# Gated linear attention and a cosine router: keys and queries in runs of two tokens, turned by small products

## The chip, the cores and the metric

The kernel runs on one core of a Trainium2 chip. The metric is device time in microseconds (us), the median of several executions; lower is better. The engines are TensorE (PE, matrix products, with its weight loads shown apart as PEld), VectorE (DVE), ScalarE (ACT), GpSimd (POOL) and SyncE (SP), which here issues DMA transfers. They run side by side, each through its own list of instructions in order, and wait for one another by semaphores.

## The reference, cut to what matters

Two blocks follow each other, all in fp32. The first is a recurrence with a decay per channel: 4 batches, 8 heads, 768 tokens, 48 channels.

```python
for t in range(S):
    state = alpha[:, :, t, :, None] * state + np.einsum('bhd,bhe->bhde', k[:, :, t], v[:, :, t])
    y[:, :, t] = np.einsum('bhd,bhde->bhe', q[:, :, t], state)
```

(The update is the outer product of k and v of the token, 48x48 for each head.) Its output, with the heads side by side, is x: 3072 tokens of 384. The second block sends each token to one of 8 experts:

```python
logits = (x / |x|) @ (expert_emb / |expert_emb|).T / tau
expert = argmax(logits);  gate = softmax(logits)[expert]
out = gate * (relu(x @ w1[expert]) @ w2[expert])      # w1 384x1024, w2 1024x384
```

## The kernel before, in words

**Stage 1** is the recurrence in 24 steps, one for each chunk of 128 tokens (6 chunks for each of 4 batches), with the loop `for s in range(NS+3)` at L756, NS being 24. Tokens lie on the 128 partitions as they come from memory. A head's 48 channels are padded to 64, so a pair of heads fills 128 rows; there are four pairs (NP). In each step:

- `load` (L448 to 465, on SP) brings alpha, k and q of chunk s+2 and v of chunk s+1. Alpha comes in two transfers, rows 1 to 112 and 113 to 127 (L454); its row 0, the token that starts a chunk, stays at the zero that POOL wrote once at the start (L226). k (L455) and q (L456) are one transfer each of 128 rows by 8 heads by 48 channels; v is three (L460, L462). All three inputs lie in memory as runs of 48 floats, 192 bytes.
- `decays` turns alpha, k and q from tokens-by-channels to channels-by-tokens, with four transposes of 128x128 each by `turned` (recorded at L193), into the PSUM tiles pa, pk and pq. DVE then scans over pa from the end of the chunk to its start, giving r (L487), and multiplies: kr = pk times r (L495, L496).
- `queries` copies pq to qc on ACT (L505). `decay_queries` has DVE scan a (L518) and POOL multiply qs = qc times a (L522); `end` (L527) is the decay over a chunk.
- `keys_back` turns kr back with four transposes into pkb, and ACT copies it to kb (L539). pa, pk, pq and pkb share one PSUM pool, ps_tr, which has three buffers.
- `scores` multiplies kr and qs of the chunk in products that use 64 rows of PE at a time (recorded at L190, tile sc); `masks` copies them to sm on ACT (L600) and POOL blanks what lies above the diagonal with two selects of 64x512, rows 0 to 63 and rows 64 to 127 (L606).
- `mix_states` and `mix_chunk` make the outputs of a chunk from state and scores (tile pyx), which ACT copies to ycols (L661); `update` adds to the state (pd, L562; DVE L570 and L572); POOL multiplies the old state by `end` (dec, L547).
- `rows` turns the outputs back to tokens and adds the router's logits in the same small products (px and pyx, operands ycols and sel, 64x56); ACT copies (L689, L692), DVE adds (L693).
- When a group of chunks is complete, `choose` and `place` find each token's expert and its row in a scratch tensor xs (DVE and PE). `to_rows` (L313) scatters a chunk's rows there by an indirect DMA of POOL, one or two chunks a step.

The steps overlap: iteration s runs keys_back, scores, masks and update of step s-1, mix_states and mix_chunk of s-2 and rows of s-3. The order of instructions on each engine is written out by hand: `in_turn()` puts what follows behind PE's last instruction in the order, `behind(s)` behind the last DVE and POOL instructions of a step, and `tc.issue_after` behind a given instruction. On PE, a step has the order pkb, pa, pk, pq, rows, scores, mix_states, mix_chunk, update.

**The end of stage 1.** When 16 chunks are routed, the expert to begin with is chosen. After the scatter of chunk 15, `fetch_early` (L176 to 185) fetches 256 of its rows (xg). `weights(0)` fetches its w1 and w2 (L140, L143, 1.5 MB each); the code puts it behind the last load of v (chunk 23), which `load(24)` issues in iteration 22. As SP ran them, the order was xg, v of chunk 23, w1, w2. `turn_early` transposes xg on PE, and `first_layer_early` multiplies w1 with it (tile phe, L710 to 718) in six batches of up to six products, between the last steps of the recurrence.

**Stage 2** runs through the experts: it fetches their rows, multiplies by w1 and w2 with a relu between, and scatters the gated result to the output. The change doesn't touch it.

Of the kernel before, what the change touches and what calls it, by code (L numbers as in the profile page):

```python
# [27 lines left out]
def kernel(  # L28
# [12 lines left out]
    nc = tc.nc  # L41
# [89 lines left out]
    w1_r = w1.rearrange("e (k p) f -> e p k f", p=P)  # L131
    w2_r = w2.rearrange("e (k p) d -> e p k d", p=P)

    def weights(i):

        e = nc.values_load(
            turn_i[0:1, i : i + 1], engines=(SP,), min_val=0, max_val=E - 1,
            skip_runtime_bounds_check_because="a sum of two experts, less E from E on",
        )
        nc.sync.dma_start(  # L140
            out=w1_s[i % NW], in_=w1_r[ds(e, 1)].rearrange("e p k f -> (e p) k f")
        )
        nc.sync.dma_start(  # L143
            out=w2_s[i % NW], in_=w2_r[ds(e, 1)].rearrange("e p k d -> (e p) k d")
        )

    def first_row(i):
        return nc.values_load(
# [25 lines left out]
    def fetch_early():  # L174

        lead = nc.values_load(  # L176
            turn_i[0:1, 0:1], engines=(SP,), min_val=0, max_val=E - 1,
            skip_runtime_bounds_check_because="a sum of two experts, less E from E on",
        )
        ins = nc.sync.dma_start(  # L180
            out=xg_s[NXG - 1][:, 0:EARLY],
            in_=xs[ds(lead * N, EARLY * P)].rearrange("(t p) r -> p t r", p=P),
        )
        tc.add_to_no_dep_group("xs", ins.ins)


    last = {}
# [11 lines left out]
    with ExitStack() as c1:  # L199
# [7 lines left out]

        NBUF, NBV = 4, 5
        at_s = [keep.tile([P, H, DP], FP32, name=f"at{i}") for i in range(NBUF)]
        qt_s = [keep.tile([P, H, DP], FP32, name=f"qt{i}") for i in range(NBUF)]  # L210
        kt_s = [keep.tile([P, H, DP], FP32, name=f"kt{i}") for i in range(NBUF)]
# [6 lines left out]

        ini_s = [keep.tile([P, NP * P], FP32, name=f"ini{i}") for i in range(2)]
        inr = keep.tile([P, NP * P], FP32, name="inr")  # L220

        def fixed_parts():
# [20 lines left out]
        a_r, q_r, k_r, v_r = (t.rearrange(chunk_of, p=P) for t in (alpha, q, k, v))  # L243


        sel = keep.tile([P, 2, NP // 2, D + E], FP32, name="sel")
# [145 lines left out]
        def counts(n):  # L392
# [32 lines left out]
            nc.vector.tensor_tensor(used, bc(r, shp, 2), bc(starts, shp, 1), ALU.is_gt)  # L425
            return nc.vector.tensor_copy(used_i, used[0:1])

        def part_of(i):
            return slice(i * HALF, (i + 1) * HALF)

# [12 lines left out]
            return pt  # L443


        AROW = P - 15

        def load(s):  # L448

            if s < NS:  # L450
                b, c = divmod(s, NCH)
                i = s % NBUF
                for p0, p1 in ((1, AROW), (AROW, P)):
                    nc.sync.dma_start(out=at_s[i][p0:p1, :, 0:D], in_=a_r[b, c, p0:p1])  # L454
                nc.sync.dma_start(out=kt_s[i][:, :, 0:D], in_=k_r[b, c])  # L455
                nc.sync.dma_start(out=qt_s[i][:, :, 0:D], in_=q_r[b, c])  # L456
            if s > 0:
                b, c = divmod(s - 1, NCH)
                vt = vt_s[(s - 1) % NBV]
                nc.sync.dma_start(out=vt[:, 0:NP, 0:D], in_=v_r[b, c][:, 0:NP])  # L460
                for i in range(2):
                    last_v = nc.sync.dma_start(  # L462
                        out=vt[part_of(i), NP:H, 0:D], in_=v_r[b, c][part_of(1 - i), NP:H]
                    )
                return last_v

        def behind(s):

            queue = ExitStack()
            for call in (*st[s]["last"], *st[s - 1].get("masked", ())):  # L470
                queue.enter_context(tc.issue_after(call.ins))
            return queue

        def decays(s):

            d = st[s]
            i = s % NBUF
            L = NP * P
            pa = turned(at_s[i], "pa")
            r = r_s[s % NR]
            nc.vector.tensor_tensor_scan(  # L487
                r[:, L - 2 :: -1], pa[:, L - 1 : 0 : -1], inr[:, L - 2 :: -1],
                1.0, ALU.mult, ALU.add,
            )  # L490
# [83 lines left out]
        def scores(s):  # L574

            d = st[s]
            kr, qs = d["kr"], d["qs"]
            for part in range(4):
                j, kh = divmod(part, 2)
                for g in range(2):  # L580
                    p, to = 2 * g + j, part_of(kh ^ g)
                    for hh in range(2):
                        sl = part_of(hh)
                        q2 = qs[sl, p].rearrange("d (h t) -> d h t", h=2)
                        if kh:
                            sc, q2 = sc_s[hh][to, 1 - g, p], q2[:, 1]
                        else:
                            sc, q2 = sc_s[hh][to, :, p], q2[:, ::-1] if g else q2
                        mm(
                            sc, lhsT=kr[sl, p, part_of(kh ^ g)], rhs=q2,  # L590
                            start=True, stop=True, skip_group_check=True,
                        )

        def masks(s):

            sm = st[s]["sm"] = work.tile([P, 2, 2, NP, HALF], FP32, name="sm")
            masked = st[s]["masked"] = []
            ready = st[s + 1]["last"] if s + 1 < NS else ()
            for hh in range(2):
                nc.scalar.copy(sm[:, hh], sc_s[hh])  # L600
            for i in range(2):
                x = sm[part_of(i), :, i].rearrange("s a p t -> s a (p t)")
                with ExitStack() as queue:
                    for call in (*ready, *masked):
                        queue.enter_context(tc.issue_after(call.ins))
                    masked.append(nc.gpsimd.affine_select(  # L606
                        out=x, in_=x, pattern=[[0, 2], [0, NP], [1, HALF]], base=0,
                        channel_multiplier=-1, compare_op=ALU.is_ge, fill=0.0,
                    ))

# [8 lines left out]
        def mix_states(s):  # L619
# [3 lines left out]
            if dec is not None:  # L623
                for q in range(NQ):
                    for j in range(2):
                        for i in range(2):
                            hh, p = i, 2 * q + (i + j) % 2
                            sl, to = slice(DP * hh, DP * hh + DP), DP * (p % 2)
# [124 lines left out]
        a0 = prepare_loads()  # L753
        prepare_fills()
        load(1)
        for s in range(NS + 3):  # L756
            if s + 2 <= NS:
                v_last = load(s + 2)
            if s + 2 == NS:

                with tc.issue_after(v_last.ins):
                    weights(0)
            if 0 <= s - 1 < NS:
                with in_turn():
                    keys_back(s - 1)
# [71 lines left out]
            with behind(s) if s < NS else tc.issue_after(st[NS - 1]["masked"][-1].ins):  # L837
                n_now = len(send) if s >= NS else 0 if s == NS - 1 else 1 + (len(send) > 2)
                for c in send[:n_now]:
                    to_rows(dest[:, c : c + 1], x_g[group_of[c]][:, c - GROUPS[group_of[c]][0]])  # L840
                    send.remove(c)
                    if c == S0 - 1:
                        fetch_early()
# [584 lines left out]
```

## Time and profile before

| | us |
|---|---|
| runs, median (lowest to highest) | 421.51 (419.65 to 422.65) |
| the profiled execution, its own time | 419.32 |
| its span, first to last instruction | 417.5 |
| PE busy, share of the span | 391.6 (94%) |
| PEld busy | 349.1 (84%) |
| DVE busy | 285.9 (68%) |
| POOL busy | 227.6 (55%) |
| ACT busy | 204.0 (49%) |
| stage 1, to PE's first phe product | 146.95 |

The shares are means over stages with different limits; matmuls are pipelined and their ends modelled, so a busy PE isn't a PE at its peak. The mean granted clock of PE is 0.991. The DMA engines moved 60.31 MB in 120150 packets, of which 103055 are under 512 bytes: nearly all of these are the 192-byte runs of stage 1. A waits line names the waiting engine, tile and line, what it waited for, and then the sum, the number of times and the longest wait in us. A timeline line gives start, duration, engine, line, operation, and output and inputs by the program's names.

### The profile page before, as it was taken

How to read it: one execution, taken by the hardware profiler on the slowest of the kernel's cores; microseconds unless marked ns; L12 is line 12 of the kernel's file. 1: busy time of each engine (PE TensorE's matmuls, PEld its weight loads, DVE VectorE, ACT ScalarE, POOL GpSimd, SP SyncE). 2: the span in 40 equal slices, each digit the busy share in tenths (PEclk: the TensorE clock that was granted, in tenths of full speed). 3: DMA queues.
4: the chain of work that ended last, by engine and by line, in shares of the span. 5: the costliest groups of instructions: out<-in, count | busy, mean ns of one | idle time of the engine just before them, and what ended most of it. 6: DMA issues, size and time to landing. Idle time of an engine off the chain costs nothing. (4 is left out here: it accounts for less than half of the span.)

```text
span 417.5 us, 13074 instructions
## 1 busy us (share of the span) xinstructions
PE 391.6 (94%) x5146; PEld 349.1 (84%) x5146; DVE 285.9 (68%) x670; ACT 204.0 (49%) x505; POOL 227.6 (55%) x276
## 2 busy tenths in 40 slices
PE   7899988989999499998999999999999999999995
PEld 6687888978888478587979979989979989979974
DVE  7888969899988314792497596693496389497530
ACT  4565455665555523552763653742661572662321
POOL 6575486777878517720681762842671492582001
PEclk9999999999999889999999999999999999999999
DMA  9988898999998795594902904703701900101001
GB/s 137 155 145 146 151 182 164 186 178 174 179 187 159 248 390 182 138 341 129 332 6 69 350 23 122 279 19 118 289 19 42 345 19 20 39 1 40 15 18 42
DMA packets 120150, 60.31 MB, mean 144 GB/s; under 512 B 103055, under 2 KB 114584, under 8 KB 120080
## 3 DMA queue, kind: packets, MB, share of 16 engines
q1 hardware_dynamic: 115976, 49.15, 48.6%
q0 software_dynamic: 3728, 10.16, 7.0%
q8 instruction: 47, 0.77, 0.8%
q14 instruction: 23, 0.19, 0.2%
q10 hardware_dynamic: 376, 0.05, 0.1%
HBM read 49.69 MB, written 11.45 MB: 146 GB/s over the span
## 5 line engine op out<-in xcount | busy, mean ns | idle before, releaser
L895 POOL DMA_INDIRECT out_dram<-y,sx x25 | 24.6, 986 | 104.6 <-DVE y L1204 42.3
L1025 DVE TENSOR_TENSOR hT<-pq,hT 128x512 f32<-128x512 f32 x63 | 43.6, 692 | 46.8 <-PE pq L1125 45.0
L1125 PE MATMUL pq<-xT_m,w_m 128*128 128x128 f32 x560 | 67.5, 275 | 0.4 <-issue 0.4
L1125 PEld LDWEIGHTS pq<-xT_m,w_m 128*128 128x128 f32 x560 | 64.8, 192 | 0.9 <-issue 0.9
L1077 POOL TENSOR_TENSOR w_m<-w_m,w 128x512 f32<-128x512 f32 x30 | 43.2, 1448 | 1.4
L522 POOL TENSOR_TENSOR qs<-qc,a 128x512 f32<-128x512 f32 x24 | 30.6, 1275 | 22.5 <-DVE a L518 14.7
L1008 PE MATMUL pyo<-w,hT 128*128 128x384 f32 x128 | 42.6, 486 | 0.0
L1125 PE MATMUL pq<-xT_m,w 128*128 128x128 f32 x280 | 38.4, 277 | 0.6
L1030 ACT ACTIVATE hT<-hT 128x512 f32<-128x512 f32 x35 | 22.1, 631 | 31.2 <-DVE hT L1025 31.2
L1125 PEld LDWEIGHTS pq<-xT_m,w 128*128 128x128 f32 x280 | 34.9, 192 | 2.1 <-issue 1.8
L1008 PEld LDWEIGHTS pyo<-w,hT 128*128 128x128 f32 x128 | 23.7, 190 | 14.8
L606 POOL TENSOR_SCALAR_AFFINE_SELECT sm<-sm 64x512 f32<-64x512 f32 x48 | 31.8, 662 | 6.6 <-DMA xs<-x,dest 4.7
L313 POOL DMA_INDIRECT xs<-x,dest x24 | 24.1, 1005 | 18.1 <-DVE x L693 11.7
L487 DVE TENSOR_TENSOR_SCAN r<-pa,inr 128x511 f32<-128x511 f32 x24 | 29.2, 1217 | 6.7 <-PE pa L193 6.5
L518 DVE TENSOR_TENSOR_SCAN a<-pa,ini 128x512 f32<-128x512 f32 x24 | 29.3, 1223 | 1.1
L190 PE MATMUL pyx<-sm,vt 128*64 128x64 f32 (+2 forms) x576 | 28.0, 243 | 1.9 <-POOL sm L606 1.9
L1197 PE MATMUL pq<-w_m,hT_m 128*128 128x192 f32 x168 | 28.4, 326 | 0.0
L190 PEld LDWEIGHTS pyx<-sm,vt 128*64 128x64 f32 (+1 forms) x576 | 24.9, 135 | 3.9 <-POOL sm L606 2.2
L1197 PEld LDWEIGHTS pq<-w_m,hT_m 128*128 128x128 f32 x168 | 27.5, 190 | 0.0
L600 ACT COPY sm<-sc 128x512 f32<-128x512 f32 x48 | 26.9, 637 | 0.4 <-PE sc L190 0.2
L689 ACT COPY lg<-pyx 128x32 f32<-128x32 f32 x24 | 4.5, 186 | 42.1 <-PE px L190 40.6
L1077 POOL TENSOR_TENSOR w_m<-w 128x512 f32<-128x512 f32 x12 | 15.3, 1276 | 15.9 <-PE pq L1125 15.9
(227 smaller groups left out, 906.5 us busy)
## 6 DMA issues: line engine op xcount, KB each, us to landing
w<-in_moe_w_dram SPq DMA_DIRECT2D x16, 1536.0 KB
kt<-in_k_dram SPq DMA_DIRECT2D x24, 192.0 KB
qt<-in_q_dram SPq DMA_DIRECT2D x24, 192.0 KB
xg<-xs SPq DMA_DIRECT2D x22, 196.5 KB
at<-in_alpha_dram SPq DMA_DIRECT2D x24, 168.0 KB
vt<-in_v_dram SPq DMA_DIRECT2D x24, 96.0 KB
vt<-in_v_dram SPq DMA_DIRECT2D x48, 48.0 KB
xg<-xs SPq DMA_DIRECT2D x8, 98.2 KB
```

Of the source, the lines that this page charges most:

```text
L190: last["pe"] = nc.tensor.matmul(*args, **kwargs)
L487: nc.vector.tensor_tensor_scan(r[:, L - 2 :: -1], pa[:, L - 1 : 0 : -1], inr[:, L - 2 :: -1], 1.0, ALU.mult, ALU.add,)
L518: d["a_scan"] = by_dve = nc.vector.tensor_tensor_scan(a, pa, ini, 0.0, ALU.mult, ALU.add)
L522: by_pool = nc.gpsimd.tensor_tensor(qs.rearrange("p n t -> p (n t)"), d["qc"], a, ALU.mult)
L600: nc.scalar.copy(sm[:, hh], sc_s[hh])
L606: masked.append(nc.gpsimd.affine_select(out=x, in_=x, pattern=[[0, 2], [0, NP], [1, HALF]], base=0, channel_multiplier=-1, compare_op=ALU. ...
L895: ins = nc.gpsimd.indirect_dma_start(out=out, out_offset=bass.IndirectOffsetOnAxis(ap=col, axis=0), in_=y, in_offset=None, bounds_check=N - 1,
L1008: pe[:] = [nc.tensor.matmul(py, lhsT=hT[:, f], rhs=w2_t[:, f], start=(f == 0), stop=(f == FT - 1),)]
L1025: dve[:] = [call(*args, **kwargs)]
L1077: by(to, x, y, op)
L1125: pe[:] = [nc.tensor.matmul(to[:, f], lhsT=left[:, f * P : (f + 1) * P], rhs=right, start=start and f == 0, stop=stop, skip_group_check=Tr ...
L1197: pe[:] = [nc.tensor.matmul(to, lhsT=left[:, f], rhs=right[:, f], start=start and f == 0, stop=stop and f == n - 1, skip_group_check=True,)]
```

## The change: what it does

- **k and q** of a chunk go into one tile `kq` of 128 rows: k on rows 0 to 63, q on rows 64 to 127, each row holding two tokens that follow each other (2t and 2t+1). In memory these two lie side by side, so a run is 96 floats. k and q stay one transfer each.
- **`turned_pair`** takes the place of the two calls of `turned` for k and q: 32 products of a 64x64 piece with the identity, for each pair of heads, each of the two tokens, k or q, and each head of the pair. A product writes 64 channels by 64 tokens into every second column of pk or pq. Both PSUM banks are allocated together ahead of the first product. The 16 rows of padding of a head then hold channels of what lies next to it, and `scores` and `mix_states` read 48 rows (`dims`) where they read 64.
- **alpha** comes in one transfer of 128 rows. Its row 0 is cleared behind the landing by a copy of zeros on ACT, `clear_first(s + 1)`, in iteration s behind the masks; that of chunk 0 ahead of the loop. POOL's clearing at the start stays.
- **The second mask** works on rows 0 to 127 with a base of 64, where it worked on rows 64 to 127 with a base of 0.
- **`weights(0)`** stands at the end of iteration 22, behind `fetch_early`: w1, then the load of v of chunk 23, then w2.

```diff
-    def weights(i):
+    def weights(i, between=None):
...
-        nc.sync.dma_start(
-            out=w2_s[i % NW], in_=w2_r[ds(e, 1)].rearrange("e p k d -> (e p) k d")
-        )
+        with tc.issue_after(between().ins) if between else ExitStack():
+            nc.sync.dma_start(
+                out=w2_s[i % NW], in_=w2_r[ds(e, 1)].rearrange("e p k d -> (e p) k d")
+            )
...
-                nc.vector.memset(kt_s[i][:, :, D:DP], 0.0)
-                nc.vector.memset(qt_s[i][:, :, D:DP], 0.0)
+                nc.vector.memset(kq_s[i][:, KQ:], 0.0)
...
+            nc.vector.memset(zero, 0.0)
...
+        q_r, k_r = (
+            t.rearrange("b h (c p two) d -> b c p h (two d)", p=HALF, two=2) for t in (q, k)
+        )
...
-                for p0, p1 in ((1, AROW), (AROW, P)):
-                    nc.sync.dma_start(out=at_s[i][p0:p1, :, 0:D], in_=a_r[b, c, p0:p1])
-                nc.sync.dma_start(out=kt_s[i][:, :, 0:D], in_=k_r[b, c])
-                nc.sync.dma_start(out=qt_s[i][:, :, 0:D], in_=q_r[b, c])
+                nc.sync.dma_start(out=at_s[i][:, :, 0:D], in_=a_r[b, c])
+                for rt, x_r in enumerate((k_r, q_r)):
+                    nc.sync.dma_start(
+                        out=kq_s[i][part_of(rt), 0:KQ].rearrange("p (h d) -> p h d", h=H),
+                        in_=x_r[b, c],
+                    )
...
+        def clear_first(s):
+
+            if s < NS:
+                nc.scalar.copy(at_s[s % NBUF][0:1, :, 0:D], zero)
...
+        def turned_pair(t):
+
+            pts = [
+                ps_tr.tile([P, NP, HALF, 2], FP32, tag="tr", name=name) for name in ("pk", "pq")
+            ]
+            with in_turn():
+                for p in range(NP):
+                    for two in range(2):
+                        for rt, pt in enumerate(pts):
+                            for hh in range(2):
+                                c0 = (4 * p + 2 * hh + two) * D
+                                mm(
+                                    pt[part_of(hh), p, :, two],
+                                    lhsT=t[part_of(rt), c0 : c0 + DP],
+                                    rhs=ident[part_of(rt), part_of(rt)],
+                                    start=True, stop=True, skip_group_check=True,
+                                )
+            return [pt.rearrange("d p t two -> d (p t two)") for pt in pts]
...
-            pk = turned(kt_s[i], "pk")
+            pk, d["pq"] = turned_pair(kq_s[i])
...
-            d["pq"] = turned(qt_s[i], "pq")
...
-                x = sm[part_of(i), :, i].rearrange("s a p t -> s a (p t)")
+                x = sm[0 : (i + 1) * HALF, :, i].rearrange("s a p t -> s a (p t)")
...
-                        out=x, in_=x, pattern=[[0, 2], [0, NP], [1, HALF]], base=0,
+                        out=x, in_=x, pattern=[[0, 2], [0, NP], [1, HALF]], base=i * HALF,
...
+        clear_first(0)
         for s in range(NS + 3):
-            if s + 2 <= NS:
-                v_last = load(s + 2)
-            if s + 2 == NS:
-
-                with tc.issue_after(v_last.ins):
-                    weights(0)
+            if s + 2 < NS:
+                load(s + 2)
...
+            if s + 1 < NS:
+                with in_turn():
+                    clear_first(s + 1)
...
+            if s + 2 == NS:
+
+                with tc.issue_after(fetched.ins):
+                    weights(0, lambda: load(NS))
```

More of the change, by code (lines that the diff above doesn't have):

```diff
@@ L184, in fetch_early @@
         tc.add_to_no_dep_group("xs", ins.ins)
+        return ins
     last = {}
@@ L209 @@
         at_s = [keep.tile([P, H, DP], FP32, name=f"at{i}") for i in range(NBUF)]
-        qt_s = [keep.tile([P, H, DP], FP32, name=f"qt{i}") for i in range(NBUF)]
-        kt_s = [keep.tile([P, H, DP], FP32, name=f"kt{i}") for i in range(NBUF)]
+        KQ = 2 * H * D
+        kq_s = [keep.tile([P, KQ + DP - D], FP32, name=f"kq{i}") for i in range(NBUF)]
         vt_s = [keep.tile([P, H, DP], FP32, name=f"vt{i}") for i in range(NBV)]
@@ L220 @@
         inr = keep.tile([P, NP * P], FP32, name="inr")
+        zero = keep.tile([1, H, D], FP32, name="zero")
         def fixed_parts():
@@ L242 @@
         chunk_of = "b h (c p) d -> b c p h d"
-        a_r, q_r, k_r, v_r = (t.rearrange(chunk_of, p=P) for t in (alpha, q, k, v))
+        a_r, v_r = (t.rearrange(chunk_of, p=P) for t in (alpha, v))
+        q_r, k_r = (
+            t.rearrange("b h (c p two) d -> b c p h (two d)", p=HALF, two=2) for t in (q, k)
+        )
         sel = keep.tile([P, 2, NP // 2, D + E], FP32, name="sel")
@@ L426, in counts, with dims @@
             return nc.vector.tensor_copy(used_i, used[0:1])
+        def dims(i):
+            return slice(i * DP, i * DP + D)
         def part_of(i):
@@ L443, in turned @@
             return pt
-        AROW = P - 15
         def load(s):
@@ L582, in scores @@
                     for hh in range(2):
-                        sl = part_of(hh)
+                        sl = dims(hh)
                         q2 = qs[sl, p].rearrange("d (h t) -> d h t", h=2)
@@ L627, in mix_states @@
                             hh, p = i, 2 * q + (i + j) % 2
-                            sl, to = slice(DP * hh, DP * hh + DP), DP * (p % 2)
+                            sl, to = dims(hh), DP * (p % 2)
                             mm(
@@ L842 @@
                     if c == S0 - 1:
-                        fetch_early()
+                        fetched = fetch_early()
+            if s + 2 == NS:
+                with tc.issue_after(fetched.ins):
+                    weights(0, lambda: load(NS))
             if s == NS:
```

## The prediction

> **What bounds the kernel now.** I read the slices of the span first, then busy time by stretches, then who waits for whom on TensorE (PE), and last PE's order of time where it stood still. The slices are 10.4 us each:
>
> ```profile
> PE   7899988989999499998999999999999999999995
> DVE  7888969899988314792497596693496389497530
> PEclk9999999999999889999999999999999999999999
> DMA  9988898999998795594902904703701900101001
> ```
>
> PE is at eight or nine tenths almost everywhere. The one hole is slice 14 (135.7 to 146.1 us), a 4, with the granted clock lower in that and the next slice. Stage 1, where all edits lie, ends there. By stretches:
>
> ```profile
> core 0: us, PE busy (x) PEld busy (x) DVE busy (x) ACT busy (x) POOL busy (x), PEclk, DMA share, GB/s
> 0.00:50.00 50.00, 44.12 (x882) 38.17 (x886) 41.82 (x100) 26.18 (x68) 30.84 (x70) 1.00 0.92 145
> 50.00:100.00 50.00, 46.26 (x1175) 42.81 (x1167) 43.02 (x97) 29.52 (x89) 37.45 (x54) 1.00 0.96 176
> 130.00:147.00 17.00, 10.45 (x295) 9.22 (x287) 8.83 (x22) 8.77 (x27) 10.22 (x18) 0.90 0.78 221
> 147.00:162.00 15.00, 15.00 (x187) 12.04 (x188) 3.50 (x20) 4.78 (x17) 5.10 (x6) 0.89 0.87 322
> ```
>
> In the loop PE and VectorE (DVE) are both nearly full, with DMA at 0.92 to 0.96 beside them; the bound changes from step to step. From 130 to 147 nobody is full: a wait sets the time. From 147 on PE has no gap, so what starts its work at 147 earlier moves the end of the kernel by as much. The waits name that start and the largest DMA wait of the mask:
>
> ```profile
> PE phe L190 <- DMA w<-in_moe_w_dram: 5.8, 1, 5.8
> PE pxe L193 <- DMA xg<-xs: 0.5, 1, 0.5
> POOL sm L606 <- DMA xs<-x,dest: 4.7, 6, 2.4
> DVE r L487 <- PE pa L193: 6.5, 14, 0.8
> ```
>
> PE lies 5.8 us idle for the first weights. Their issue stands behind the last values in SyncE's (SP) list:
>
> ```profile
> 134.95 0.40 SPq L180 DMA_DIRECT2D xg<-xs  x1
> 135.45 1.74 SPq L460 DMA_DIRECT2D vt<-in_v_dram  x1
> 137.28 1.28 SPq L462 DMA_DIRECT2D vt<-in_v_dram  x2
> 139.09 0.39 SPq L140 DMA_DIRECT2D w<-in_moe_w_dram  x1
> ```
>
> **Weights ahead of values.** w1(0) takes the place of v(23): issue 135.45 instead of 139.09, -3.64 us. From issue to PE's first product it took 7.86 us (146.95); kept, the product comes at 143.31. PE's own work before it ends at 140.95 (32 score products from 140.31), so the gap shrinks from 6.0 to 2.4 us and some of it stays. The three loads of v(23) now stand behind w1; mix_chunk(23) needs them at 156.1, and issued some 0.5 us later than w1 with w1's 4.6 us of packets ahead they land near 143: hidden. w2 moves from 139.68 to about 139.6 behind them and is first read at 165.6; xg keeps its place.
>
> The first six phe products ran at 0.43 us apart, 2.83 us in all, the next six in 1.48; the granted clock is 0.90 from 130 to 147 and 0.89 from 147 to 162. If the shorter gap keeps the clock, that is -1.35; if not, 0. I take -1.35: in the loop PE's gaps reach 1.8 us (at 86) and the granted clock of that stretch is 1.00. [...]
>
> **Upper mask on all rows.** The mask on rows 64 to 127 waited 4.7 us in six places for the landing of the scatter before it; the mask on rows 0 to 63 and the 128-row operations of GpSimd (POOL) between never did. From row 0 the wait should go. The mask's own cost stays: 0.66 us on 64x512, and a memset takes 0.52 on one partition as on 128. The largest wait (2.35, at 85.3) lies beside a run of DVE that sets that step, so it gives 0; the one at 129.5 (0.63) holds the last scatter before xg (issued 130.48), so xg, w1 and the first product come 0.6 earlier: -0.6, bounds 0 and -0.6. With it the gap is 1.8.
>
> **Products for transposes.** Per step 8 transposes of 128x128 (0.109 us apart, 0.87 in all for pk and pq) become 32 products of 64x64. The rows of the same kind are px and pyx (64x56): 32 PE instructions, so two to a product, in 0.51 us, a group of four every 0.058. 64 instructions make 0.93 us, +0.06 against 0.87. The 64x64 scores go at 0.056 to 0.058 a group too. The stride of two in the PSUM write has no row: below, 0.056 (0.90); above, the transposes' 0.109 a group, 1.74. I take 0.93, the same mode and size. [...]
>
> Both banks are wanted up front. ps_tr has three buffers: pkb, pa and pk stand in them now and pq waits for pkb to be copied out (kb). A step on PE without other waits (from 59.39): pkb 0.49, pa 0.44, pk 0.44, pq 0.56, rows 0.51, scores 0.69, mix_states 0.49, mix_chunk 0.94, update 0.64, 5.2 us. kb starts 0.69 after pkb and takes 0.59, so the bank is free 1.36 after pkb's start; pk begins at 0.93 now, pq at 1.37, just hidden. The pair begins at 1.36 and ends at 2.29; rows begins at 1.93 now. That is +0.36 us of PE in the 17 steps that have pkb in this pool, +0.06 in the other seven: 6.5 us. It counts only where PE sets the step. A DVE step is 4.2 to 4.5 us and choose adds 3.2, so pairs with a choose are DVE's (the scans of r at 60.52 and 71.99 are 11.5 us apart against 10.4 of PE) and hide it. Left are nine steps at 0.36 (1 to 4, 8, 9, 20, 21, 23) and two at 0.06: +3.4; bounds 0 and +6.5. qc is 0.36 later; qs waits for the scan of a as well (14.7 us in ten places), which hides that. Scores and mix_states contract 48 rows instead of 64, which I cost at nothing: 64 columns take 0.217 us through 64 rows and 0.222 through 128. The memsets at the start (eight become five, on DVE) stand beside the load of alpha.
>
> **Loads.** k and q go in runs of 384 B: 4096 packets of 192 B a step become 3072. A 192 B packet took 15 ns, one of 1536 B 65: the line gives 23 for 384 (bounds 15 and 30), so per step 3.84 us of the 16 engines becomes 3.37, -12%, and SP's issues go from 7 to 6. PE's waits for late k, q, alpha and v sum to 6.5 us in the steps that PE sets (1, 2, 3, 5, 7, 9, 20, 22, 23). I take 5 of it as gone, -5; bounds 0 and -6.5. Behind it DVE's choose is late next, so no more than that.
>
> Alpha's row 0 is now cleared on ScalarE (ACT): 24 copies of 1x384. An ACT copy of 128x384 took 0.48, 8x192 0.40, so 12 us of ACT, bounds 9.6 and 12.5; in a step it lies between sm and ycols. ACT is idle for 23.8 of the first 50 us and 20.5 of the next, and it stood 1.55 us before kb at 60.1 but only 0.41 before kb at 127.6: there 0.1 of it delays kb and the pair, which in all 17 steps would be +1.7; I take 0, since most steps have more. It waits for alpha to land 0.7 us before pa needed it, and ycols, kb and rows' copies queue behind: cost 0 if alpha is in time (issue to landing 4.6 to 5.9 us, issued almost two steps ahead), the lateness otherwise. The first load of alpha now overlaps POOL's clearing of row 0 (L226), which ends at 1.97: issue 0.8 becomes 2.0, +1.2 at the start.
>
> **Sum.** Loop: +1.2 +3.4 -5 = -0.4 (bounds -5.3 and +9.4, not all at once). Tail: -3.64 -0.6 -1.35 = -5.6. In all -6.0. The profiled execution took 419.32 us: 413.3 in its frame. It lies 2.2 under the median of the runs, 421.51; in the frame of the runs the prediction is 415.5.
>
> **The rivals.** What a measurement of this kernel can tell from no change is about 1%, 4.2 us.
>
> First, slower: the strided write doubles a group. For it: no row of before has a strided PSUM write. Against: the rows' groups fill the same quadrants at 0.058. Place: the pair, in all 24 steps. At 0.109 a pair takes 1.74, the step grows by 1.17 and sets every step, choose pairs too (12.6 against 11.9): 24 x 6.3 is 151 us where the loop now takes 132, +19, and -5.6 gives 435. It decides from where the tail's gain is used up: 5.6/24 more than the loop's 5.5 us a step, so a PE step of 5.7, a pair of 1.1, a group of 0.07.
>
> Second, the same: PE's +6.5 is absorbed nowhere and DMA's lateness stays half: 1.2 +6.5 -3.3 -4.2 (the tail without the clock) = +0.2, 421.7.
>
> Third, the change doesn't do what it says: w1 still comes late, since its expert's number or xg's wait holds SP, or the products wait for xg. For it: xg was landing at 139.0. Against: SP issued xg at 134.95 and v directly behind. Only the loop's -0.4 remains: 421.
>
> Fourth, slower: ACT's clearing waits for late alpha. At 0.5 us in each of 20 steps it is +10 -6 = 426.
>
> Fifth, more: DMA lateness goes whole and PE's +0.36 is hidden by the pair's overlap with the copies: -1.5 -3.4 on top, 410.6.
>
> **How the numbers follow.** Forecast 0.50 (411 to 419; of it 0.42 below 417.3), second 0.17, first 0.15, fifth 0.08, fourth 0.06, third 0.04. Faster by over 1%: 0.42 + 0.08 = 0.50. Within: 0.08 + 0.17 + 0.04 = 0.29. Slower: 0.15 + 0.06 = 0.21. The range leaves out the first and some of the fifth: 409 to 427.
>
> **What would show it.** w1 issued right behind xg and PE's gap ahead of phe at about 1.8 us; six phe products in 1.5; no wait of sm for xs; pk and pq at 0.058 a group, starting when kb ends; row-0 copies of 0.5 us on ACT without a wait for alpha; r's scan waiting less for pa. It would be wrong if the group takes 0.07 or more, or if ycols waits behind the clearing.

## The result, and the profile after

The changed kernel took 440.76 us (median of 4 runs, 439.08 to 441.82), the kernel before 420.73 on the same chip. The ratio is 1.048, with a 95% interval of 1.044 to 1.051: 20 us slower, where 415.5 was predicted. The execution profiled took 441.31 us with a span of 439.5; the one of before had a span of 417.5, so 22.0 us are to be found between the two traces.

The slices of the span, 11.0 us each, for the kernel after:

```profile
span 439.5 us, 15733 instructions
PE   4888889897997988999999999999999999999994
DVE  3775776869686890379349669679269269669440
PEclk8699999998999996999999999999999999999999
DMA  8988657678576165859590380540730550100101
```

The hole ahead of the first expert is gone (slice 16, from 164.8 us on, is an 8 on PE), and DMA has fallen to five to eight tenths after the first slices. But stage 1 lasts into slice 16 (phe at 173.05 us), where before's ended at the start of its slice 15 (146.95 us), and PE starts with a 4 and a row of eights. The kernel has 2659 instructions more. The same by stretches:

```profile
core 0: us, PE busy (x) PEld busy (x) DVE busy (x) ACT busy (x) POOL busy (x), PEclk, DMA share, GB/s
0.00:50.00 50.00, 36.60 (x1000) 32.76 (x1002) 29.65 (x73) 23.47 (x56) 25.29 (x62) 0.90 0.91 156
50.00:100.00 50.00, 44.89 (x1493) 40.74 (x1487) 38.02 (x84) 29.84 (x87) 31.44 (x44) 1.00 0.68 153
```

In the loop all of PE, DVE and DMA are less busy than before (PE 46.26, DVE 43.02, DMA 0.96 from 50 to 100). Nobody is the bound, so somebody waits. PE's waits from 10 to 172 us name it, or rather don't (waiting engine, tile and line, what released it; sum, times and longest in us):

```profile
PE pyx L192 <- issue: 5.4, 3, 3.5
PE pa L195 <- ACT at L479: 5.0, 1, 5.0
PE sc L192 <- issue: 4.3, 5, 1.1
PE pq L192 <- issue: 2.8, 2, 1.9
PE pd L192 <- issue: 2.7, 2, 1.7
PE pyx L192 <- POOL x L889: 1.5, 1, 1.5
PE pk L192 <- issue: 1.4, 3, 0.9
```

"issue" is time in which PE waited for nothing that the profile shows: 16.6 us in these lines, in five different kinds of product. In before's trace the same view, from 10 to 139 us, has one line of this kind:

```profile
PE pd L190 <- issue: 0.8, 2, 0.5
```

One of the stops after is in the midst of a run of scores (from the order of time on PE):

```profile
57.43 0.34 PE L192 MATMUL sc<-qs,kr 48*64 48x64 f32 x8 [1.00 <-issue]
```

The other large line is the start: pa waits 5.0 us for the clearing of alpha's row.

**What "issue" stands for here.** The trace also has PE's instruction packets, 16384 bytes each, on a queue of their own. The profile's page counts them for the whole execution; before and after:

```profile
q8 instruction: 47, 0.77, 0.8%
```

```profile
q8 instruction: 58, 0.95, 0.9%
```

Number the rows of PE and PEld, their sequencer's included, in order of time, and set each stop (from start to start of two matmuls) beside the last packet that landed before it (worked out from the trace of after):

```
row of the stop   stop, us   packet from - to       PE goes on    after its end
     705            1.25      23.17 -  24.70            25.99          1.29
     962            1.22      28.30 -  29.22            30.83          1.62
    1217            0.44      32.58 -  34.08            35.66          1.58
    1473            1.92      37.48 -  39.25            40.62          1.36
    1730            1.35      42.84 -  44.21            45.46          1.24
    1986            0.46      47.45 -  48.37            49.65          1.27
    2242            0.62      50.77 -  51.73            53.34          1.61
    2497            1.27      54.59 -  56.09            57.43          1.34
    ...
    8642            3.78     164.41 - 165.39           166.77          1.38
```

The stops lie 256 rows apart or a multiple of it, give or take one, whatever product stands there, and each ends 1.2 to 1.65 us after a packet. So each packet goes with 256 rows of PE's program, a block below. That PE stands still because it has used up the instructions that it has is the author's reading of these distances and times; the runs below test it. In all there are 18 such stops of 0.4 us or more ahead of phe, 21.9 us when a normal distance of 0.1 is taken off each; before had 4, 2.6 us. (Here and below a stop is counted when it stands at such a boundary and ends at most 1.75 us after a packet.)

**Why now.** A full step of before has some 278 rows on PE, one of after 389: eight transposes of one matmul and one weight load each became 32 products of two and two, +112. A step without waits, from 153.35 on, takes 5.44 us, that is 3.6 us for a block. The packets came every 4.48 us on average (31 intervals from 18.09 to 157.10), but this is the loop's own pace, one packet for each block, and no limit by itself. The limit shows in the way round: the second to eighth stop of the table end 3.7 to 5.0 us after PE had crossed the boundary before. The packet started 1.1 to 2.3 us behind that crossing, was on its way for 0.9 to 1.8, and PE went on 1.2 to 1.6 after it. A block of 3.6 us is shorter than that. What makes a packet start when it does, no run shows.

**Where the 22.0 us are.**

| | before | after | difference |
|---|---|---|---|
| first transpose of alpha (pa of chunk 0) | 4.70 | 9.88 | +5.2 |
| stops at block boundaries, ahead of phe | 2.6 | 21.9 | +19.3 |
| from pkb to rows, a step with pkb and no stop | 1.93 | 2.14 to 2.21 | +0.2 to 0.3 a step, an estimate of 5 to 7 in 24 steps |
| PE's wait for w1 ahead of phe | 5.8 | 0 | -5.8 |
| rest of stage 1 | | | some 0 to 2 |
| **phe's first product** | 146.95 | 173.05 | **+26.1** |
| from phe to the end | 270.6 | 266.5 | -4.1 |

The rest holds two things that work against each other. PE's waits for other engines and for DMA, from 10 to 139 us and without the late start, fell from 7.4 to 4.7 us. And the longest stops cost more than their own length: beside them the granted clock is 0.50, for 20.5 us of stage 1 in all (from 8.63 to 18.87, from within the late start on; 107.61 to 111.03, at the end of the stop of 2.11 us; 165.64 to 172.47, from within the one of 3.78 on), and before for 3.5 (from 143.44 on, in the wait for w1). That the stops bring the lower clock is the author's reading of these places. The stretch that holds the last of these, after:

```profile
165.00:180.00 15.00, 13.23 (x205) 11.22 (x205) 1.70 (x8) 5.70 (x18) 3.95 (x8) 0.77 0.55 172
```

From the end of that stop to phe PE took 6.28 us, and 3.75 for the same products in the run with the first weights late (below, 169.15 to 172.90), where the clock stayed at 1.00.

### The profile page after: what moved, and what is told of

Read it like the earlier page. It is cut to its first block, busy times and chain, and to the rows that moved or that the text cites. A ratio compares the mean times of both kernels' runs of the same rounds, so it can differ in the third digit from the quotient of the medians.

```text
span 439.5 us, 15733 instructions
## 1 busy us (share of the span) xinstructions
PE 404.9 (92%) x6490; PEld 363.5 (83%) x6490; DVE 286.1 (65%) x667; ACT 214.4 (49%) x529; POOL 225.2 (51%) x276
## 5 line engine op out<-in xcount | busy, mean ns | idle before, releaser
L192 PE MATMUL pk<-ident,kq 64*64 64x64 f32 x768 | 34.4, 234 | 1.4 <-issue 1.4
L192 PEld LDWEIGHTS pk<-ident,kq 64*64 64x64 f32 x768 | 29.9, 142 | 5.7 <-issue 5.6
L192 PE MATMUL pq<-ident,kq 64*64 64x64 f32 x768 | 31.3, 233 | 2.8 <-issue 2.8
L638 POOL TENSOR_SCALAR_AFFINE_SELECT sm<-sm 64x512 f32<-64x512 f32 (+1 forms) x48 | 30.8, 660 | 5.3 <-ACT sm L632 5.3
L192 PE MATMUL pyx<-sm,vt 128*64 128x64 f32 (+2 forms) x576 | 30.2, 247 | 2.6 <-POOL x L889 1.5
L192 PEld LDWEIGHTS pyx<-sm,vt 128*64 128x64 f32 (+1 forms) x576 | 26.9, 139 | 4.7 <-POOL x L889 1.7
L192 PEld LDWEIGHTS pq<-ident,kq 64*64 64x64 f32 x768 | 27.3, 145 | 3.7 <-issue 3.4
L192 PE MATMUL sc<-qs,kr 48*64 48x128 f32 (+1 forms) x768 | 24.8, 251 | 4.3 <-issue 4.3
```

What stands on the lines that cost most here:

```text
L192: last["pe"] = nc.tensor.matmul(*args, **kwargs)
L638: masked.append(nc.gpsimd.affine_select(out=x, in_=x, pattern=[[0, 2], [0, NP], [1, HALF]], base=i * HALF, channel_multiplier=-1, compare_ ...
```

## The experiments

The runs fell on several chips, and on most of them the kernel before takes 430 us, not 421. Every ratio is to the kernel before on the same chip; times of stage 1 are compared within a chip where not said otherwise. Numbers of lines differ a little from kernel to kernel.

### Half of the pair's instructions, the same columns

```diff
-                    for two in range(2):
+                    for two in range(1):
...
-                                    pt[part_of(hh), p, :, two],
+                                    pt[part_of(hh), p],
...
-                                    rhs=ident[part_of(rt), part_of(rt)],
+                                    rhs=bc(ident[part_of(rt), part_of(rt)], [HALF, HALF, 2], 2),
```

> The changed kernel with 16 products of 128 columns in place of 32 of 64 in the pair: the same columns through PE, half of the pair's instructions. It leaves out the odd tokens of k and q (each holds its neighbour's values), so the routing and with it stage 2 may differ: stage 1 counts. Instruction fetch says that the stalls at block boundaries (22 us in the changed kernel) fall to under 8 us and stage 1 ends 10 to 18 us earlier than the changed kernel's 173 us. The rival (the pair's array time, the bank wait behind kb and the later order of kr and qs) says no change, within 3 us.

Measured: the stops at block boundaries are 4, 3.3 us, and the first transpose of chunk 23 comes at 141.54 where the changed kernel had it at 159.29; phe at 152.00 for 173.05. A full step has some 326 rows there, and the ones without waits take 5.44 us, that is 4.3 us for a block. What is left of PE's waits, from 10 to 150 us:

```profile
PE pa L195 <- ACT at L479: 4.9, 1, 4.9
PE pyx L192 <- DVE at_row L369: 1.8, 3, 0.7
PE pyx L192 <- issue: 1.6, 2, 1.0
PE sc L192 <- issue: 1.1, 2, 0.9
```

The issue lines have gone from 16.6 to 2.7 us; the late start stays. The ratio, 1.022 (1.016 to 1.027), has another routing in it. Those two traces are of different chips, so the pair was run again beside the changed kernel:

> The changed kernel with 16 products of 128 columns for 32 of 64 once more, beside the changed kernel on the same chip; it leaves out the odd tokens of k and q, so the routing and stage 2 may differ. Instruction fetch says that chunk 23's first transpose comes 12 to 20 us earlier than in the changed kernel and that the stalls at block boundaries fall by 10 us or more; the rival (array time and order) says within 3 us.

> The changed kernel once more, as the measure for the three runs beside it on the same chip: 4.4 to 5.2% above the kernel before.

Measured: the changed kernel 1.061 (1.055 to 1.066), more than expected, chunk 23 at 163.18, 11 stops of 14.1 us; with half of the instructions 1.041 (1.032 to 1.050), chunk 23 at 150.14, 2 stops of 2.0 us. Chunk 23 comes 13.0 us earlier. The stops ahead of it are 9.3 us and 2.0, so 7.3 of the 13.0 are stops; the changed kernel's longest, 4.8 us, lies behind chunk 23, and phe comes 18.6 us earlier (178.39 and 159.75). The pair's own time is not quite equal: from pkb to rows it is 2.05 us with half of the instructions, 2.14 to 2.21 with all, an estimate of 2 to 4 us in 24 steps. What is left of the 13.0 isn't taken apart. And once more without alpha's part, the products held in one order:

```diff
-            with in_turn():
-                for p in range(NP):
+            for p in range(NP):
...
+                            with in_turn():
                                 mm(
```

> The changed kernel with alpha as before (two loads, no clearing), and the products of the pair held in the order pk, pq, pk, pq as the changed kernel runs them. Instruction fetch says that the stalls stay, 12 to 22 us, and that the time is 3 to 12 us above the weights-and-mask run beside it. The rival (the loss is alpha's part) says within 3 us of it or below.

> The run pair_in_turn with 16 products of 128 columns for 32 of 64; it leaves out the odd tokens of k and q, so the routing and stage 2 may differ and stage 1 counts. Instruction fetch says that chunk 23's first transpose comes 8 to 18 us earlier than in pair_in_turn. The rival says within 3 us.

> The kernel before with w1 ahead of the last values alone, once more: 3 to 6 us faster than before.

Measured, on one chip: chunk 23 at 143.75 with the weights alone, 156.91 with the pair, 149.94 with half of its instructions; ratios 0.998 (0.993 to 1.003), 1.038 (1.030 to 1.046) and 1.018 (1.011 to 1.026). The stops are 1.6, 11.4 and 3.9 us. The weights alone, of which 3 to 6 us of gain were expected, gained nothing that can be told from none. At the end the pair lies 16.7 us above them, and 18.4 above the run with weights and mask on this chip (mask_2, below: 428.92 us, chunk 23 at 140.24), which is nearer to it, since it has the mask's edit as well. Both are more than expected. Of the 13 to 17 us that the pair costs in stage 1 some 7 go with half of its instructions (a little under the 8 expected at least). What stays, 6 to 10, isn't taken apart: 0.12 us a step from pkb to rows (2.05 for 1.93) and 2.3 us of stops are part of it. Three pairs of traces agree in kind: with half of the instructions for the same columns, most of the stops are gone and stage 1 is 7 to 18 us shorter at chunk 23.

### Instructions without work: a miss

```diff
+                for j in range(n):
+                    hh = j % 2
+                    mm(
+                        pt[part_of(hh), j : j + 1], lhsT=t[0:HALF, hh],
+                        rhs=ident[0:HALF, 0:1],
+                        start=True, stop=True, skip_group_check=True,
+                    )
```

> The kernel before with 28 products of 64x64 by one column in each step ahead of the transposes of q; their results are written over by these. They add as many PE instructions as the pair does (56 matmuls and 56 weight loads a step) and nothing to loads, banks or other engines. Instruction fetch says slower than before by 10 to 20 us, with stalls at boundaries of 256 instructions. The rival (order, banks, copies) says slower only by the products' own time, under 0.4 us in those of the 24 steps that PE sets, 2 to 8 us.

Measured: 446.84 us, ratio 1.058 (1.053 to 1.064): slower by 25 us, more than was said, and for another reason. The trace is of the longest of its runs, 452.38 us. The 28 products of one column took 1.75 us a step, 0.0625 each (pq to rows 2.31 us where a step of before has 0.56). All use the same 64 rows, and one takes about as long as a whole group of four in px (0.058 us). A step of 390 rows became 6.97 us, that is 4.6 us for a block of 256, and there was 1 stop in stage 1, 2.5 us at its very end. That bounds the pace from the other side: at 3.6 us a block PE had 18 stops, at 4.6 one. As a test of the theory it failed, since it slowed PE to a pace at which the stops are nearly gone.

### The parts alone

```diff
-            pk = turned(kt_s[i], "pk")
+            pk, d["pq"] = turned_pair(kq_s[i])
...
-            d["pq"] = turned(qt_s[i], "pq")
```

(with the loads of k and q as in the change; the rest as before)

> The kernel before with the loads of k and q in runs of two tokens and the pair of products alone; alpha, masks and weights stay. The theory (PE's instruction fetch: blocks of 256 PE instructions, 16384 bytes, that the pair uses up faster than they come) says slower than before by 12 to 20 us, with PE standing still about 1.2 to 1.6 us behind the end of an instruction packet a dozen times or more. The rival (alpha's clearing on ScalarE and its late first load make the loss) says within 4 us of before.

Measured: 430.41 us, ratio 1.019 (1.010 to 1.028); chunk 23 at 150.74 for 132.94 in before's trace, and 7 stops of 6.5 us. Less than expected, and by an order of products that the change doesn't have: the planner, which orders what the code leaves open, put the 16 products of pk ahead of the 16 of pq, so that products next to each other all read the same 64 rows of kq, and the pair took 1.52 us where the changed kernel's takes 1.12 to 1.19. From pkb to rows it is 2.54 us for before's 1.93, an estimate of 15 us in 24 steps, so most of the 17.8 us at chunk 23 is the slower pair, with fewer stops beside it. This run doesn't measure the change's pair; the run with the order held does.

```diff
-                for p0, p1 in ((1, AROW), (AROW, P)):
-                    nc.sync.dma_start(out=at_s[i][p0:p1, :, 0:D], in_=a_r[b, c, p0:p1])
+                nc.sync.dma_start(out=at_s[i][:, :, 0:D], in_=a_r[b, c])
...
+                nc.scalar.copy(at_s[s % NBUF][0:1, :, 0:D], inr[0:1] ...)
```

> The kernel before with alpha in one load and its row 0 cleared on ScalarE alone (the zeros come from the tile of the scan's restarts, whose row 0 holds them). The first load of alpha stands late in SyncE's list here too, as in the changed kernel: the start's theory says 4 to 8 us slower than before at chunk 0, of which some comes back over DMA; 2 to 6 us slower at the end. The rival, that clearing costs nothing and the start is made good by step 4 as the prediction had it, says within 2 us of before.

> The kernel before with alpha in one load, cleared on ScalarE, and POOL's clearing at the start cut to the padding, so that alpha of chunk 0 is first in SyncE's list. If the loss of alpha alone (3.4%) was the late first load and its order in the list, this is within 1% of before or faster; if it was ScalarE waiting for alpha with its other copies behind it, it is 2 to 4% slower still, with ScalarE's waits for alpha summing to 10 us or more.

Measured: 1.034 (1.028 to 1.041) alone, 12 us where 2 to 6 were expected, and 1.029 (1.021 to 1.037) with alpha first in SyncE's list again. So the late start isn't the reason here (chunk 0 at 13.80 and at 7.49, but chunk 23 at 157.22 and 156.33). With alpha first, the stops at boundaries sum to 0.5 us and ACT's waits say where the time went:

```profile
ACT at L467 <- DMA at<-in_alpha_dram: 21.7, 13, 3.9
```

and PE's, what stood behind the clearing on ACT:

```profile
PE pq L193 <- ACT kb L541: 5.9, 5, 2.5
PE p L193 <- ACT qc L507: 4.4, 1, 4.4
```

This is the prediction's fourth rival. In the changed kernel it is nearly absent (1.6 us, 2 times): there DMA is at 0.68, not 0.96, and kb stands ahead of the clearing. Two parts that each cost 2 to 4% alone gave 4.8% together, through different waits.

The weights and the mask:

> The kernel before with w1 of the first expert ahead of the last values alone. The prediction's term says faster by 3.6 to 5 us: w1 issued at 135.5 instead of 139.1, phe at 142 to 143.5 instead of 146.95, its first batch in about 1.5 us instead of 2.8. The rival (w1 comes no earlier, or what is gained is given back in the second layer) says within 2 us of before.

> The kernel before with w1 ahead of the last values and the second mask on all rows; loads, transposes and alpha stay. The prediction's terms say 415 to 417, 0 to 1 us below the weights alone (416.2), with no wait of the mask for a scatter's landing. The rival (the mask's wait was beside other work) says the same time as the weights alone within 1 us.

> The kernel before with w1 ahead of the last values and the second mask on all rows, beside the weights alone on one chip: if the mask's wait for the scatter held the end of stage 1, 0.5 to 2 us below weights_2; if other work covered it, within 1 us of it, either sign.

Measured: the weights alone 416.23 us, 0.986 (0.981 to 0.991), on a chip where before takes 421; 0.998 (0.993 to 1.003) on one where it takes 430. With the mask 0.998 (0.993 to 1.002) and 0.999 (0.995 to 1.004) on two chips of the latter kind. On the first chip the prediction's term (-3.6 to -5) about holds in the time (-5.3), though its profiled execution (span 418.1) shows little of it: w1 followed xg by 0.94 us, not 4.14, but xg itself was 1.5 later; phe came at 146.04 and its first batch took 2.63 us, behind 2.9 us of idle PE (3.1 from start to start). On the other chips the gain can't be told from nothing. The mask's waits for a scatter's landing are gone with the edit (2.3 us in 4 places with the weights alone, none with the mask), and the time doesn't show it. No version of these is faster than the kernel before on every chip it ran on.

### The start, and VectorE's order

```diff
-                nc.gpsimd.memset(at_s[i][0:1], 0.0)
+                nc.gpsimd.memset(at_s[i][0:1, :, D:DP], 0.0)
```

> The changed kernel with POOL's clearing at the start cut to the padding of row 0, so that no transfer of alpha overlaps it; alpha of chunk 0 is then first in SyncE's list again. The theory says that the first transposes of alpha come at 5 to 6.5 us instead of 9.9 and that 3 to 5 us of it reach the end: 436 to 438. The rival (the loop's stalls at instruction blocks take it back, since the first blocks then come as late as now) says within 2 us of the changed kernel, 439 to 442.

> The changed kernel with alpha of chunk 0 first in SyncE's list, once more beside the changed kernel itself. If the late first load counts to the end, 3 to 5 us below it; if the instruction blocks of the loop take the start's gain back (PE reaches the block boundaries earlier but the blocks come at their own pace), less than 1.5 us.

Measured: 1.047 (1.037 to 1.056) on one chip; on another 1.049 (1.040 to 1.059) beside 1.061 (1.055 to 1.066) for the changed kernel itself, 450.38 and 454.48 us. There chunk 0 comes at 5.85 for 10.10 and chunk 23 at 158.90 for 163.18: the 4.3 us at the start are still there 23 steps later. In this pair of traces the loop neither makes the start good nor takes it back (the intervals of the two ratios overlap a little). The prediction had its 1.2 us at the start count to the end; that the start is made good by step 4 stands in the expectation for alpha alone, and not in it.

```diff
-            d["a_scan"] = by_dve = nc.vector.tensor_tensor_scan(
-                a, pa, ini, 0.0, ALU.mult, ALU.add
-            )
+            with tc.issue_after(d["kr_last"].ins):
+                d["a_scan"] = by_dve = nc.vector.tensor_tensor_scan(
+                    a, pa, ini, 0.0, ALU.mult, ALU.add
+                )
```

In the changed kernel VectorE runs the scan of a ahead of the products kr; before it ran them the other way round.

> The changed kernel with alpha first (as in the run beside it) and, besides, VectorE's scan of a held behind the two products kr, the order that they have in the kernel before. If the later kr holds PE's transposes of the next step, this is 3 us or more below the run with alpha first alone; if instruction blocks set the loop, within 2 us of it or slower, since qs comes later.

Measured: 1.044 (1.038 to 1.050), beside 1.047 with the changed kernel's order; the intervals lie over one another. The order isn't the cause.

### Fewer data packets beside the instruction packets

```diff
-            if s > 0:
+            if 0 < s <= NBV or s == NS:
```

> The changed kernel with v loaded for the first five chunks and the last only; the others use old values, so the outputs and the routing differ and stage 1 alone counts. Per step it takes away 1024 of some 4100 packets of 192 or 384 bytes. If the instruction blocks come late because their packet waits among the data, the stalls at block boundaries (22 us in the changed kernel) fall below 14 and stage 1 gets shorter by as much. If the block's own round trip sets it, they stay within 3 us of 22.

Measured: 10 stops of 10.8 us where the run with alpha first, on the same chip, has 15 of 16.6. The stops of the loop fall. The packets of instructions are as long on their way (1.11 and 1.13 us on average), but start sooner behind a boundary (median 1.2 and 1.7 us), so some of their lateness may be the data's. Against that, stage 1 got no shorter (chunk 23 at 161.05 and 161.70, the first with the late start), and 5.4 us of the 10.8 are the one stop at row 8642. How much of a packet's lateness is waiting among data isn't settled.

### The first weights, and the longest stop

> The changed kernel with the first weights behind the last values, as before. If the weights' packets held the instruction block at the end of stage 1, PE's stop there (3.8 us ahead of mix_states, block boundary 8642 by index) falls below 1.5 us, and in its place PE waits 3 us or more for w1 ahead of phe. If the block comes late by itself, the stop stays at 3 us or more.

Measured: 1.045 (1.036 to 1.053). The stop at row 8642 (3.78 us in the changed kernel, 3.81 to 5.45 in four other runs with w1 ahead of the values, 2.37 in pair_in_turn) is 0.73 us; mix_states and mix_chunk pass there with 0.47 us idle between:

```profile
168.03 0.66 PE L190 MATMUL pyx<-qs,dec 48*64 48x128 f32 x15
169.15 0.32 PE L190 MATMUL pyx<-qs,dec 48*64 48x128 f32 x1 [0.47 <-issue]
172.12 0.86 PE L190 MATMUL sc<-qs,kr 48*64 48x128 f32 x32
172.90 0.48 PE L190 MATMUL phe<-exT,w 128*128 128x256 f32 x1
```

and phe follows the scores without a wait although w1 was issued behind the values, at 165.65. The half of the expectation that PE would then wait for w1 is wrong: in a loop this slow the weights are in time either way. Part of the stop only moved: one block later, behind the first six phe products, PE was idle for 1.48 us at 176.32, 1.4 us after a packet. In the changed kernel w1 was issued at 158.04 and its packets ran from 159.6 to 165; the packet of instructions that PE wanted started at 164.41. The early weights gained nothing there, and the one stop of 3.78 us goes with them. Two more runs fit. With VectorE's order changed, w1 was early too, but the packet started at 162.54, ahead of most of w1's, and there was no stop. In the run with instructions without work, where the weights stand as before, w1's packets still ran when the packet was due (it started at 174.03), and its one stop, 2.5 us, is there. The comparison of the times themselves is across chips and left open.

## Why the prediction was wrong

The first rival was the slower one that it had in mind, a strided PSUM write, and not the one that came. By its own steps:

- **Products for transposes.** The array's time was right: a group of four every 0.058 us at the stride of two, as for px; pq begins when kb's bank comes free, 1.33 us after pkb (1.36 was worked out), and rows 2.14 to 2.21 after it (2.29). +0.2 to 0.3 a step for +0.36. The stride cost little or nothing (pk and pq 235 and 234 ns a product, scores of 64 columns without a stride 222; a group 0.058 us, not the 0.109 of the first rival). The step that failed is the sentence "64 instructions make 0.93 us": it counted their time on the array and not their number, some 389 rows on PE in a full step for 278. The profile's page showed the queue of 47 packets of instructions, and before's trace has four stops at the same spacing of 256 rows. That row was missing from the sum: +19.3 us, of which 3.7 is the one stop behind w1.
- **Loads.** Packets of 384 B took 22 ns in the median (23 worked out; its two rows give 22), and DMA's share fell from 0.96 to 0.68. But the 5 us of gain weren't there: the waits that named an input DMA summed to 1.7 us (pq, pk and pa), and of the 6.5 us put down to lateness 2.4 were stops for instructions, the waits of pd at 36.00, 46.97 and 58.78. A gap with a DMA running beside it was read as a gap because of it.
- **Alpha.** +1.2 us at the start was right in kind and wrong in size, +5.2: the planner put both chunks' k and q ahead of the load of alpha that now has to wait for POOL, and it was issued at 5.42 where 2.0 was predicted:

```profile
0.83 0.77 SPq L462 DMA_DIRECT2D kq<-in_k_dram  x1
1.65 0.62 SPq L462 DMA_DIRECT2D kq<-in_q_dram  x1
2.31 0.69 SPq L462 DMA_DIRECT2D kq<-in_k_dram  x1
4.71 0.60 SPq L462 DMA_DIRECT2D kq<-in_q_dram  x1
5.42 1.18 SPq L460 DMA_DIRECT2D at<-in_alpha_dram  x2
```

  The late start isn't made up later (the 4.3 us at chunk 0 that alpha first saves are 4.3 at chunk 23). The clearing itself took 0.507 us (0.5 predicted) and waited for alpha twice.
- **Weights ahead of values.** The mechanism was right: w1 was issued 0.94 us behind xg, in place of 4.14, phe followed the scores at once and its first six products took 1.49 us, not 2.83. But that the clock's term came out (-1.35, on the prediction's assumption that a gap of 2.4 us keeps the clock) is luck. In the changed kernel the half clock lay ahead of phe, behind the stop for instructions, and was over at 172.47; with the weights alone, behind 2.9 us of idle PE, the six took 2.63; and a stop of 2.11 us in the changed kernel's loop has 3.4 us at 0.50 behind it. From phe to the end 4.1 us were gained, 1.5 of them ahead of the second layer. What the sum missed is the packet of instructions that came among w1's (164.41, w1's from 159.6 to 165), with 3.78 us of stop, 0.73 where the weights stand behind the values.
- **Mask.** No wait of sm for a scatter is left in the changed kernel. Its 0.6 us couldn't be seen in any time.
- **Rivals.** Second to fifth: the fourth is shown for alpha alone and is small in the change; the third fell, since w1 came early; the second and fifth fell with the size of the loss.

## What to carry to other kernels

Count an engine's instructions, not only their time. Where a part becomes many short ones, work out how long PE takes for 256 of them and set it beside the packets in the trace: here 4.6 us a block ran almost without stops, and 3.6 lost 0.4 to 2.1 us, once 3.8, at half of the boundaries. A wait named "issue" at even distances in instructions was that here, and with a large load, w1, started ahead of its time one of them was 3.78 us, for 0.73 with the load as before. A wait added to the first transfer of a loop can move the whole list behind it; look at the order that comes out, not at the wait alone.

## What the runs showed of the hardware

The stops 256 rows of PE apart, above (18 of them, 21.9 us, each ending 1.2 to 1.65 us after a packet of 16384 bytes), are the first thing. The second isn't explained. On the chips where the kernel before takes 430 us, PE stops for about 0.6 us, three or four times in a row, 0.72 to 0.76 us apart, in the small products and from about 57 us on, with nothing that released it and a granted clock of 1.00. In the run weights_2, whose stage 1 is before's but for the weights, such stops end at 56.98, 57.72 and 58.48, at 81.51 and 82.25, at 120.68, 121.46 and 122.19; they don't follow packets of instructions (the one at 81.51 is at a boundary of 256 rows, but 3.7 us after a packet). Each run on these chips has 11 to 19 stops of 0.4 us or more ahead of phe that no engine released and that don't follow a packet of instructions at a boundary, 5.5 to 9.8 us in all, whatever the kernel; the runs where before takes 421 us have none. Chunk 23 comes at 143.75 there (7.4 us of such stops) and at 134.54 in the same kernel on the chip where before takes 421. The changed kernel's loss holds on both kinds (1.048 and 1.061); the weights' gain was seen on the one kind only.
